# Three products of an expert in a row, and its weights split two stages ahead

## Chip, core and metric

One Trainium2 chip, of which the kernel uses one core. The metric is the device time of one execution in microseconds, lower is better. PE is the matmul engine (TensorE), ACT the ScalarE, DVE the VectorE, POOL the GpSimd; SP issues most of the DMAs.

## What is computed

Causal attention with a decay (4 batches, 8 heads, 576 positions of 64), then a dense layer pair, then a layer of 8 experts of which each token uses one. Only the last part is touched:

```python
e_idx = np.argmax(x @ w_gate, axis=1)          # x: 2304 x 512, 8 experts
for e in range(E):
    mask = e_idx == e
    h = np.maximum(x[mask] @ w1[e], 0.0)       # w1: 8 x 512 x 1024
    ye = h @ w2[e]                             # w2: 8 x 1024 x 512
    out[mask] = gate_w[mask, None] * eom[mask, e, None] * ye
```

## The kernel before

All matrices are held as a pair of 16-bit parts, high and low, so a product of two takes three matmuls for each 128x128 step. A float32 weight is brought in by SP (L867, tile `stw`, 512 KB, an eighth of an expert's weights: four for W1, four for W2), and *split*: ACT copies the high part (L879), DVE subtracts to get the low part (L880).

The experts' part works on lists of tokens, 128 to a block. An expert has up to three blocks in the first round. Block 0 of experts 0 and 1 is a reserved block that is done early, ahead of `round_`, with its operands and results in the tile `wi` of the dense layer, which is free by then (L1128 to L1132, L1158). For all others `gather` (L942) lets POOL fetch the rows of a block from DRAM into `xg` (L951, indirect DMA, three buffers), and SP transposes them into `xs` by DMA (L954, two buffers). `expert1` (L964), the first product, makes eight groups of 12 matmuls (L977), each in a PSUM bank; ACT (L980) and DVE (L981) evacuate a group into `hT`. The main blocks use the pool `ps2` with five banks, the third block `ps_mm` with three. `expert2` (L985), the second product, takes 24 matmuls of 512 columns for each block (L996), ACT scales the result into `y` (L1002), and POOL scatters it to the output (L1003, indirect DMA).

The third block (block 2) is done only if the expert has over 256 tokens (`when`, a branch at run time); in these inputs experts 0, 1, 4 and 6 have it. A second round for over 384 tokens does not run.

The order on PE, ACT and DVE is that of the code (`manual_schedule`); POOL and SP get theirs from the scheduler. `round_` runs the first product of expert e+1 (with its third block's both products), then gathers for e+2, then the second product of e. `weights_steps` (L844) is a generator: a step splits one part and issues the load three parts on (the ring `stw` has three buffers in the pool `wp`). `spread` takes such steps between the groups of a product, and what is left behind it. 16 parts, all weights of experts 0 and 1, are split ahead of `round_`. `xp` (L1165) is the pool of the experts' part; it opens where the dense layer's tiles close, so its tiles lie where those lay, and the framework makes their first users wait for the last users of what lay there.

Of the kernel before, what the change touches and what calls it, by code (L numbers as in the profile page):

```python
# [9 lines left out]
F32 = mybir.dt.float32  # L10
# [8 lines left out]
P = 128  # L19
# [39 lines left out]
def attention_moe_kernel(ctx: ExitStack, tc: tile.TileContext, q, k, v, f, w_in, w_out,  # L59
# [5 lines left out]
    E, _, F2 = w1.shape  # L65
    KD = DM // P
# [255 lines left out]
    st = {}  # L322
# [518 lines left out]

    def weights_steps(wp):  # L844

        parts, tiles = [], {}

        def add(e, which):
            wv = (w1, w2)[which][e].rearrange("(k p) f -> p k f", p=P)
            for i in range(KD):  # L850
                n = F2 // P // KD
                parts.append((wv[:, i] if which == 0 else wv[:, n * i:n * i + n], e, which,
                              i if which == 0 else slice(n * i, n * i + n)))

        for e, which in ((0, 0), (1, 0), (0, 1), (1, 1)):
            add(e, which)
        for e in range(2, E):
            add(e, 0)
            add(e, 1)
        sts = []  # L860

        def fetch():
            st = wp.tile([P, F2], F32, tag="stw", name="stw", bufs=3)
            src = parts[len(sts)][0]
            if len(src.shape) == 3:
                st = st.rearrange("p (a b) -> p a b", a=src.shape[1])
            nc.sync.dma_start(out=st, in_=src)  # L867
            sts.append(st)

        for _ in range(3):  # L870
            fetch()
        yield
        for i, (_, e, which, js) in enumerate(parts):
            if (e, which) not in tiles:
                tiles[e, which] = (wp.tile([P, 2, KD, F2], F16, tag="W1", name="W1", bufs=2) if which == 0 else
                                   wp.tile([P, 2, F2 // P, DM], F16, tag="W2", name="W2", bufs=2))
                wts[e, which] = tiles[e, which]
            hi, lo = (tiles[e, which][:, x, js] for x in range(2))
            nc.scalar.activation(out=hi, in_=sts[i], func=AF.Copy)  # L879
            nc.vector.tensor_tensor(out=lo.bitcast(BF16), in0=sts[i], in1=hi, op=ALU.subtract)  # L880
            if len(sts) < len(parts):
                fetch()
            yield
# [58 lines left out]
    def gather(e, pool, blocks, into=None):  # L942

        n = len(blocks)
        if into is None:
            xs = pool.tile([P, 2 * KD, NSB * P], F16, tag="xs2", name="xs2", bufs=2)[:, :, 0:n * P]
            xg = [pool.tile([P, 2 * DM], F16, tag="xg", name="xg", bufs=3) for _ in blocks]
        else:
            xs, xg = into[0], [into[1]]
        for j, s in enumerate(blocks):  # L950
            nc.gpsimd.indirect_dma_start(out=xg[j], out_offset=None,  # L951
                                         in_=rows[0:NT if into is None else NBL * P, :],
                                         in_offset=bass.IndirectOffsetOnAxis(ap=slot[s][0][:, e:e + 1], axis=0))
            nc.sync.dma_start_transpose(out=xs[:, :, j * P:(j + 1) * P], in_=xg[j])  # L954
            xs_t[e, s] = (xs, j * P)

    def h_tile(e, blocks, into=None):
        n = len(blocks)
        if into is None:
            into = xp.tile([P, F2 // P, 2, NSB * P], F16, tag="hT", name="hT", bufs=2)  # L960
        for j, s in enumerate(blocks):
            h_t[e, s] = (into, j * P)

    def expert1(e, ps_pool, blocks):  # L964

        W1, (xs, o) = wts[e, 0], xs_t[e, blocks[0]]
        hT, ho = h_t[e, blocks[0]]
        w = len(blocks) * P
        hs = slice(ho, ho + w)
        for m in range(F2 // P):  # L970
            ps = ps_pool.tile([P, 512], F32, tag="mm", name="mm")
            i = 0
            for j in range(KD):
                for a, b2 in ((0, 0), (0, 1), (1, 0)):
                    l = W1[:, a, j, m * P:(m + 1) * P]
                    r = xs[:, b2 * KD + j, o:o + w]
                    nc.tensor.matmul(ps[:, 0:w], lhsT=l.bitcast(BF16) if a else l, rhs=r.bitcast(BF16) if b2 else r,  # L977
                                     start=i == 0, stop=i == 3 * KD - 1)
                    i += 1
            nc.scalar.activation(out=hT[:, m, 0, hs], in_=ps[:, 0:w], func=AF.Relu)  # L980
            nc.vector.scalar_tensor_tensor(out=hT[:, m, 1, hs].bitcast(BF16), in0=ps[:, 0:w], scalar=0.0,  # L981
                                           in1=hT[:, m, 0, hs], op0=ALU.max, op1=ALU.subtract)
            yield

    def expert2(e, pool, ps_pool, blocks, into=None):  # L985

        W2 = wts[e, 1]
        NF2 = F2 // P
        for s in blocks:
            hT, ho = h_t[e, s]  # L990
            ps = ps_pool.tile([P, 512], F32, tag="mm", name="mm")
            i = 0
            for m in range(NF2):
                for a, b2 in ((0, 0), (0, 1), (1, 0)):
                    l, r = hT[:, m, a, ho:ho + P], W2[:, b2, m, :]
                    nc.tensor.matmul(ps, lhsT=l.bitcast(BF16) if a else l, rhs=r.bitcast(BF16) if b2 else r,  # L996
                                     start=i == 0, stop=i == 3 * NF2 - 1)
                    i += 1
                if m % 2 and m < NF2 - 1:
                    yield  # L1000
            y = pool.tile([P, DM], F32, tag="y", name="y", bufs=3) if into is None else into
            nc.scalar.activation(out=y, in_=ps, func=AF.Copy, scale=slot[s][2][:, e:e + 1])  # L1002
            nc.gpsimd.indirect_dma_start(out=out,  # L1003
                                         out_offset=bass.IndirectOffsetOnAxis(ap=slot[s][1][:, e:e + 1], axis=0),
                                         in_=y, in_offset=None, bounds_check=NT - 1, oob_is_err=False)
            yield


    def run(g, n=1):

        last = None
        for _ in range(n):
            r = next(g, "end")
            last = r or last
            if r == "end":
                break
        return last
# [10 lines left out]
    def adv():  # L1028
        with tc.high_priority(offset=ATTN_FIRST):
            r = next(at, "end")  # L1030
        nsteps[0] += 1
        return r != "end"
# [33 lines left out]
    wp = None  # L1066
    nw = 0

    def open_weights():
        nonlocal wp, wg_  # L1070
        while adv():
            pass
        attn_ctx.close()
        wp = ctx.enter_context(tc.tile_pool(name="wp", bufs=1, side="right"))
        wg_ = weights_steps(wp)

    for c in range(NCH):
# [13 lines left out]
        for _ in moe1_steps(c):  # L1091
# [24 lines left out]
            if c == NCH - 2 and wp is None and len(complete) == 3 * B:  # L1116
                open_weights()
# [21 lines left out]
    ps2 = ctx.enter_context(tc.tile_pool(name="ps2", bufs=5, space=PSUM))  # L1139

    first = [expert1(e, ps2, (0,)) for e in range(2)]
# [21 lines left out]
            more = nc.values_load(nrounds[0:1, 0:1], min_val=0, max_val=NT // CAP)  # L1163
    moe1_ctx.close()
    xp = ctx.enter_context(tc.tile_pool(name="xp", bufs=1))  # L1165

    def round_(first):
        main = [(1,) if first and e < 2 else (0, 1) for e in range(E)]

        def fetch(e):  # L1170
            blocks = main[e] + (2,)
            gather(e, xp, blocks)
            h_tile(e, blocks)

        def when(e):

            return tc.If(regs[e] > CAP - P) if first else nullcontext()

        def spread(g, n):

            done = 0
            for i, _ in enumerate(g):
                if done < n and i % 2 == 0:
                    run(wg)
                    done += 1
            run(wg, n - done)

        def first_product(e):
            spread(expert1(e, ps2, main[e]), KD if 1 < e else 0)
            with when(e):  # L1190
                for _ in expert1(e, ps_mm, (2,)):
                    pass
                for _ in expert2(e, xp, ps_mm, (2,)):
                    pass

        wg = wg_
        if not first:
            wg = weights_steps(wp)
            run(wg, 4 * KD + 1)
        fetch(0)  # L1200
        fetch(1)
        first_product(0)
        for e in range(E):
            if e + 1 < E:
                first_product(e + 1)
            if e + 2 < E:
                fetch(e + 2)
            spread(expert2(e, xp, ps2, main[e]), KD if e + 2 < E else 0)
# [41 lines left out]
```

## Time and profile before

| | us |
|---|---|
| median of 3 runs (824.41 to 963.61) | 827.16 |
| the profiled execution | 825.52 |
| its span | 823.7 |
| PE busy in it | 741.9 (90%) |
| ACT, DVE, POOL busy | 452.1, 467.9, 313.7 |

The span is the time from the first to the last instruction that the profile shows. The timeline merges neighbouring instructions of one kind into a row, so that a row is a stage or a piece of one; where an engine stood before a row, brackets give how long and what ended the wait. The experts' part begins at 606.85 us, and PE's last matmul there ends near 812.

### The profile page before, as it was taken

Reading aid. Unit: us, or ns where it says so; the run is one execution under the profiler, and the core shown is the slowest. Engines: PE = TensorE matmul, PEld = TensorE weight load, DVE = VectorE, ACT = ScalarE, POOL = GpSimd, SP = SyncE. Lnnn points to the kernel's source line nnn. Section 1 sums busy time; section 2 is a strip of 40 time slices with the busy share of each in tenths; the row PEclk is TensorE's granted clock in tenths of the full one; section 3 lists DMA queues with packets and bytes.
Section 4 is the critical chain, followed back from the end, with each engine's and each line's share of the span. In section 5 each row is a group of like instructions: output and inputs, shape, how many; then the busy total and the mean of one; then the engine's idle time right before and its main releaser. Section 6 shows DMA issues by size and latency. Waiting matters only on the chain. (4 is left out here: it accounts for less than half of the span.)

```text
span 823.7 us, 16593 instructions
## 1 busy us (share of the span) xinstructions
PE 741.9 (90%) x6177; PEld 476.7 (58%) x6177; DVE 467.9 (57%) x1267; ACT 452.1 (55%) x909; POOL 313.7 (38%) x393
## 2 busy tenths in 40 slices
PE   4755988979899999998999999999999879999994
PEld 2543455645566655565555666666877546767561
DVE  7998988548642864258524776750512455455330
ACT  4874879757883775378615655540222445455330
POOL 9546788855663453156413500010131222211101
PEclk9876999999999999999999999999999989999998
DMA  8758899989994783579524757511364798599411
GB/s 245 233 177 188 177 218 255 193 133 174 171 167 104 149 140 66 93 136 161 92 46 104 122 173 237 150 37 39 82 163 90 226 284 256 173 271 247 146 55 40
DMA packets 263778, 127.95 MB, mean 155 GB/s; under 512 B 214658, under 2 KB 247522, under 8 KB 263684
## 3 DMA queue, kind: packets, MB, share of 16 engines
q1 hardware_dynamic: 251860, 105.20, 58.3%
q0 software_dynamic: 4960, 15.73, 6.0%
q10 hardware_dynamic: 6864, 5.80, 2.6%
q8 instruction: 54, 0.88, 0.4%
q14 instruction: 40, 0.33, 0.1%
HBM read 71.52 MB, written 10.08 MB: 99 GB/s over the span
## 5 line engine op out<-in xcount | busy, mean ns | idle before, releaser
L695 PE MATMUL mm<-xT,wi 128*128 128x384 f16 (+1 forms) x1152 | 208.6, 328 | 8.2 <-DMA xT<-xn 5.0
L718 PE MATMUL mm<-g,wo 128*128 128x384 f16 (+1 forms) x1152 | 198.3, 326 | 1.5 <-DVE hr L702 1.4
L695 PEld LDWEIGHTS <-wi 128*128 128x128 f16 (+1 forms) x1152 | 110.5, 98 | 82.3 <-issue 13.0
L718 PEld LDWEIGHTS <-wo 128*128 128x128 f16 (+1 forms) x1152 | 111.0, 98 | 74.7 <-issue 3.8
L880 DVE TENSOR_TENSOR W<-stw,W 128x1024 bf16<-128x1024 f32 x64 | 77.7, 1224 | 68.5 <-ACT W L879 64.5
L977 PEld LDWEIGHTS <-W 128*128 128x128 f16 (+1 forms) x1344 | 100.7, 99 | 22.8 <-DVE W L880 5.4
L977 PE MATMUL mm<-xs,W 128*128 128x256 f16 (+3 forms) x1152 | 102.6, 250 | 9.1 <-ACT W L879 4.0
L394 POOL TENSOR_TENSOR pn<-ms,pn 128x384 bf16<-128x384 f32 (+1 forms) x80 | 82.7, 1039 | 56.1 <-ACT pn L393 50.7
L376 ACT ACTIVATE ms<-ms,nm 128x512 f32<-128x512 f32 (+4 forms) x144 | 79.5, 577 | 39.1 <-DVE nm L342 27.9
L996 PE MATMUL mm<-W,hT 128*128 128x512 f16 (+1 forms) x432 | 94.5, 379 | 0.6 <-PEq L1190 0.3
L879 ACT ACTIVATE W<-stw 128x1024 f16<-128x1024 f32 x64 | 66.6, 1052 | 30.4 <-DMA stw<-in_moe_w_dram 29.8
L342 DVE CUSTOM_DVE_ANT_1 ms<-sc,mask 128x128 f32<-128x128 f32 (+3 forms) x128 | 59.1, 484 | 26.2 <-PE sc L295 13.9
L707 DVE TENSOR_TENSOR g<-hr,g 128x384 bf16<-128x384 f32 x80 | 55.6, 697 | 32.0 <-ACT g L703 31.9
L996 PEld LDWEIGHTS <-hT 128*128 128x128 f16 (+1 forms) x432 | 41.8, 98 | 50.7 <-issue 1.6
L702 DVE SCALAR_TENSOR_TENSOR hr<-hr,mm 128x384 f32<-128x384 f32 x96 | 52.7, 549 | 27.9 <-ACT hr L699 27.4
L699 ACT ACTIVATE hr<-mm,bias 128x384 f32<-128x384 f32 x96 | 54.5, 568 | 17.8 <-PE mm L695 16.2
L703 ACT ACTIVATE g<-hr 128x384 f16<-128x384 f32 x96 | 49.4, 516 | 26.7 <-DVE hr L702 26.1
L1003 POOL DMA_INDIRECT out_dram<-y,ids x18 | 18.3, 1014 | 120.2 <-ACT y L1002 104.0
L981 DVE SCALAR_TENSOR_TENSOR hT<-mm,hT 128x128 bf16<-128x128 f32 (+1 forms) x96 | 32.9, 355 | 47.0 <-ACT hT L980 32.7
L428 PE MATMUL pv<-vt,pt 128*128 128x65 f16 x320 | 41.5, 197 | 18.4 <-DVE xs L453 9.9
L295 PE MATMUL sc<-K,q 128*128 128x256 f16 (+3 forms) x192 | 49.0, 297 | 7.6 <-DVE nm L342 7.0
L980 ACT ACTIVATE hT<-mm 128x128 f16<-128x128 f32 (+1 forms) x96 | 30.8, 329 | 42.0 <-PE mm L977 37.6
(189 smaller groups left out, 1121.3 us busy)
## 6 DMA issues: line engine op xcount, KB each, us to landing
stw<-in_moe_w_dram SPq DMA_DIRECT2D x64, 512.0 KB
wo<-in_moe_w_in_dram SPq DMA_DIRECT2D x16, 512.0 KB
raw<-in_moe_w_out_dram ACTq DMA_DIRECT2D x11, 512.0 KB
rows<-rw POOLq DMA_DIRECT2D x15, 256.0 KB, 3.6
ldk<-in_k_dram SPq DMA_DIRECT2D x14, 256.0 KB
ldq<-in_q_dram SPq DMA_DIRECT2D x14, 256.0 KB
ldv<-in_v_dram SPq DMA_DIRECT2D x13, 256.0 KB
g<-in_moe_w_out_dram SPq DMA_DIRECT2D x3, 512.0 KB
```

Source lines behind the costliest of these rows:

```text
L342: nc.vector.tensor_tensor_reduce(out=pairs(ms[:, off:off + w]), in0=ps[:, 0:w].rearrange("p (c j) -> p c j", c=2), in1=pairs(mask[:, 640 - ...
L376: nc.scalar.activation(out=ms[:, off:off + w], in_=ms[:, off:off + w], func=AF.Exp, scale=-1.0, bias=nm[:, i:i + 1])
L394: nc.gpsimd.tensor_tensor(out=lo.bitcast(BF16), in0=ms[:, 0:N], in1=hi, op=ALU.subtract)
L695: nc.tensor.matmul(ps[:, 0:w], lhsT=l.bitcast(BF16) if a else l, rhs=r.bitcast(BF16) if b2 else r, start=i == 0, stop=i == 3 * KD - 1)
L699: nc.scalar.activation(out=hr, in_=ps[:, 0:w], func=AF.Relu, bias=bias3)
L702: nc.vector.scalar_tensor_tensor(out=hr, in0=hr, scalar=6.0, in1=ps[:, 0:w], op0=ALU.min, op1=ALU.mult)
L707: either.tensor_tensor(out=g[:, m, 1, 0:w].bitcast(BF16), in0=hr, in1=g[:, m, 0, 0:w], op=ALU.subtract)
L718: nc.tensor.matmul(ps[:, 0:w], lhsT=l.bitcast(BF16) if a else l, rhs=r.bitcast(BF16) if b2 else r, start=i == 0, stop=i == 3 * NF - 1)
L879: nc.scalar.activation(out=hi, in_=sts[i], func=AF.Copy)
L880: nc.vector.tensor_tensor(out=lo.bitcast(BF16), in0=sts[i], in1=hi, op=ALU.subtract)
L977: nc.tensor.matmul(ps[:, 0:w], lhsT=l.bitcast(BF16) if a else l, rhs=r.bitcast(BF16) if b2 else r, start=i == 0, stop=i == 3 * KD - 1)
L996: nc.tensor.matmul(ps, lhsT=l.bitcast(BF16) if a else l, rhs=r.bitcast(BF16) if b2 else r, start=i == 0, stop=i == 3 * NF2 - 1)
```

## The change

The loads' ring is kept outside the generator: `stw_in` names a pool and a number of buffers, `wp` and 3 at first, `xp` and 4 from the opening of `xp` on. At the start of round one two more loads are issued, so five parts are under way or waiting. In `round_` each expert's first product, third block and second product follow one another, and the splits are taken from the first product of expert 1 on, to that of expert 6.

```diff
+    stw_in, fetches = [], []
+
     def weights_steps(wp):
...
         def fetch():
-            st = wp.tile([P, F2], F32, tag="stw", name="stw", bufs=3)
+            pool, bufs = stw_in
+            st = pool.tile([P, F2], F32, tag="stw", name="stw", bufs=bufs)
...
         for _ in range(3):
             fetch()
+        fetches.append(fetch)
         yield
...
         wp = ctx.enter_context(tc.tile_pool(name="wp", bufs=1, side="right"))
+        stw_in[:] = wp, 3
         wg_ = weights_steps(wp)
...
     xp = ctx.enter_context(tc.tile_pool(name="xp", bufs=1))
+    stw_in[:] = xp, 4
...
         def first_product(e):
-            spread(expert1(e, ps2, main[e]), KD if 1 < e else 0)
+            spread(expert1(e, ps2, main[e]), KD if 0 < e < E - 1 else 0)
...
         fetch(0)
         fetch(1)
-        first_product(0)
+        for _ in range(2 if first else 0):
+            fetches[0]()
         for e in range(E):
-            if e + 1 < E:
-                first_product(e + 1)
+            first_product(e)
             if e + 2 < E:
                 fetch(e + 2)
             spread(expert2(e, xp, ps2, main[e]), KD if e + 2 < E else 0)
```

On POOL, this is the order at the start of round one before; `out_dram<-wi` is the scatter of a reserved block (expert 0, then expert 1), `xg<-rows` a gather:

```order
L793 DMA rows<-wi 128x1024 x3
L951 DMA xg<-rows,ids 128x1024 x6
L1003 DMA out_dram<-wi,ids 2304x512
L951 DMA xg<-rows,ids 128x1024
L1003 DMA out_dram<-wi,ids 2304x512
L1162 TENSOR_LOAD cnt
```

And with the change, at the same place, in a list that also names what each waits for (DMASW is a completed DMA of POOL's, DMAHW one of SP's):

```order
L1007 DMA out_0_dram<-wi_98,ids_7779 2304x512 [waits DVE_49,Activation_49]
L1007 DMA out_0_dram<-wi_98,ids_7779 2304x512 [waits DMASW4_49,Activation_49]
L955 DMA xg_8588<-rows_100,ids_8297 128x1024 [waits DMASW3_49,DMASW5_49,DMASW2_49,DMASW7_49,DMASW1_49,DMAHW4_49,DMASW0_49,DMAHW5_49,DVE_49,PE_49]
L955 DMA xg_8589<-rows_100,ids_8297 128x1024
L955 DMA xg_8596<-rows_100,ids_8297 128x1024
L955 DMA xg_8597<-rows_100,ids_8297 128x1024 [waits DMAHW5_49,DMASW6_49]
```

Six gathers stood ahead of the first scatter and one between the two; now both scatters stand ahead of all gathers, and the second scatter waits for the first (DMASW4).

On SP, at the start of round one before (`xs<-xg` are the transposes):

```order
L1163 ISA x2
L954 DMA_TRANSPOSE xs_8587<-xg 128x8x128 x2
L954 DMA_TRANSPOSE xs_8595<-xg 128x8x128 x2
L1190 COMPARE_AND_BRANCH
L1190 UNCONDITIONAL_BRANCH x2
L954 DMA_TRANSPOSE xs_9145<-xg 128x8x128 x3
```

And with the change:

```order
L1168 ISA x2
L870 DMA stw<-in_moe_w_dram 128x1024
L870 DMA stw<-in_moe_w_dram 128x2x512 x3
L958 DMA_TRANSPOSE xs_8587<-xg 128x8x128 x2
L958 DMA_TRANSPOSE xs_8595<-xg 128x8x128 x2
L1196 COMPARE_AND_BRANCH
L1196 UNCONDITIONAL_BRANCH x2
L958 DMA_TRANSPOSE xs_8878<-xg 128x8x128 x3
L870 DMA stw<-in_moe_w_dram 128x2x512
L870 DMA stw<-in_moe_w_dram 128x1024 x2
```

Four loads now stand ahead of the first transposes.

On ACT, from the third block of expert 0 on, before (`hT` is an evacuation of a first product, `y` of a second one, `W<-stw` a split):

```order
L980 ACTIVATE hT<-mm 128x128 x8
L1002 ACTIVATE y<-mm,cf 128x512
L1190 UNCONDITIONAL_BRANCH x2
L980 ACTIVATE hT<-mm 128x128 x8
L1190 COMPARE_AND_BRANCH
L980 ACTIVATE hT<-mm 128x128 x8
L1002 ACTIVATE y<-mm,cf 128x512
L1190 UNCONDITIONAL_BRANCH x2
L879 ACTIVATE W_9163<-stw 128x1024 x2
L1002 ACTIVATE y<-mm,cf 128x512
L879 ACTIVATE W_9163<-stw 128x1024 x2
L980 ACTIVATE hT<-mm 128x256
```

And with the change:

```order
L1006 ACTIVATE y<-mm,cf 128x512
L1196 UNCONDITIONAL_BRANCH x2
L883 ACTIVATE W_8896<-stw 128x1024 x2
L1006 ACTIVATE y<-mm,cf 128x512
L883 ACTIVATE W_8896<-stw 128x1024 x2
L984 ACTIVATE hT<-mm 128x128
L883 ACTIVATE W_8951<-stw 128x1024
L984 ACTIVATE hT<-mm 128x128 x2
L883 ACTIVATE W_8951<-stw 128x1024
L984 ACTIVATE hT<-mm 128x128 x2
L883 ACTIVATE W_8951<-stw 128x1024
L984 ACTIVATE hT<-mm 128x128 x2
```

Expert 0's second product with its four splits now stands ahead of expert 1's first product, and that has four splits of its own among its eight groups. Up to the scatters of the reserved blocks, no engine's order differs but in line numbers.

## Rows read from the trace of the kernel before

**Rows 1.** Timeline of PE, 560 to 640: start, length, line, operation, count, idle time before.

```profile
606.85 11.31 PE L977 MATMUL mm<-xs,W 128*128 128x128 f16 x192
617.99 5.34 PE L996 MATMUL mm<-W,hT 128*128 128x512 f16 x24
623.17 4.41 PE L977 MATMUL mm<-xs,W 128*128 128x128 f16 x76
```

**Rows 2.** Timeline of PE, 630 to 823.

```profile
635.89 10.52 PE L996 MATMUL mm<-W,hT 128*128 128x512 f16 x48
646.25 0.82 PE L977 MATMUL mm<-xs,W 128*128 128x256 f16 x6
...
661.29 5.34 PE L996 MATMUL mm<-W,hT 128*128 128x512 f16 x24 [0.15 <-PEq L1190]
666.47 0.82 PE L977 MATMUL mm<-xs,W 128*128 128x256 f16 x6
...
672.59 11.50 PE L977 MATMUL mm<-xs,W 128*128 128x256 f16 x85 [0.66 <-DVE W L880]
684.24 10.52 PE L996 MATMUL mm<-W,hT 128*128 128x512 f16 x48 [0.15 <-PEq L1190]
694.60 16.09 PE L977 MATMUL mm<-xs,W 128*128 128x256 f16 x192
...
726.06 10.64 PE L977 MATMUL mm<-xs,W 128*128 128x256 f16 x96
...
747.21 1.15 PE L977 MATMUL mm<-xs,W 128*128 128x256 f16 x9
...
764.76 15.70 PE L996 MATMUL mm<-W,hT 128*128 128x512 f16 x72
```

**Rows 3.** Groups by line, 600 to 823: busy us, mean ns, idle before by releaser.

```profile
L977 PE MATMUL mm<-xs,W 128*128 128x256 f16 (+3 forms) x1152 | 102.6, 250 | 9.1 <-ACT W L879 4.0 <-DVE W L880 3.6 <-issue 1.3
...
L880 DVE TENSOR_TENSOR W<-stw,W 128x1024 bf16<-128x1024 f32 x48 | 58.3, 1224 | 59.6 <-ACT W L879 55.8 <-issue 3.1 <-DVEq L1190 0.6
...
L981 DVE SCALAR_TENSOR_TENSOR hT<-mm,hT 128x128 bf16<-128x128 f32 (+1 forms) x96 | 32.9, 355 | 47.0 <-ACT hT L980 32.7 <-ACT wi L1002 11.3 <-issue 1.7
```

**Rows 4.** Stretches of 2 us: PE, PEld, DVE, ACT, POOL busy, PEclk, DMA share, GB/s.

```profile
674.00:676.00 2.00, 2.00 (x12) 1.35 (x10) 0.80 (x1) 1.44 (x2) 0.00 (x0) 0.50 1.02 379
676.00:678.00 2.00, 2.00 (x16) 1.62 (x15) 0.77 (x3) 0.42 (x2) 0.00 (x0) 0.79 0.91 339
```

**Rows 5.** Timeline of POOL, 578 to 660.

```profile
595.17 0.99 POOL L951 DMA_INDIRECT xg<-rows,ids  x1 [2.69 <-ACT wi L980]
...
603.70 0.94 POOL L951 DMA_INDIRECT xg<-rows,ids  x1 [5.01 <-DMA xs<-xg]
...
607.61 1.02 POOL L1003 DMA_INDIRECT out_dram<-wi,ids  x1 [0.30 <-issue]
611.76 0.97 POOL L951 DMA_INDIRECT xg<-rows,ids  x1 [3.13 <-DMA out_dram<-wi,ids]
...
650.83 0.97 POOL L951 DMA_INDIRECT xg<-rows,ids  x1 [2.40 <-DMA xs<-xg]
```

**Rows 6.** Timeline of ACT, 600 to 823.7.

```profile
607.05 0.69 ACT L1002 ACTIVATE wi<-mm,cf 128x512 f32<-128x512 f32 x1 [5.18 <-issue]
...
641.86 1.99 ACT L879 ACTIVATE W<-stw 128x1024 f16<-128x1024 f32 x2
```

**Rows 7.** DMA issues, 595 to 700: count, median us from issue to landing.

```profile
xg<-rows,ids POOLq DMA_INDIRECT x19, 5.7
...
out_dram<-wi,ids POOLq DMA_INDIRECT x2, 4.0
```

**Rows 8.** Landing of all 20 scatters to the output.

```profile
DMA to landing us min/median/max: 2.7/3.0/4.0
```

**Rows 9.** Timeline of SP's queue, 578 to 660.

```profile
598.56 40.14 SPq L954 DMA_TRANSPOSE xs<-xg  x9
...
644.59 1.25 SPq L954 DMA_TRANSPOSE xs<-xg  x1
```

## Prediction

> **What bounds the kernel now.** I read the page first and then only the last quarter of the span, since nothing before the experts' part differs in the order of any engine. The page gives a span of 823.7 us; the execution's own time is 825.52, beside a median of 827.16. From 606.85 on, PE does nothing but experts 0 to 7, and its timeline shows them one behind the other [rows 1, 2]. A first product over two blocks is 96 matmuls of 128x256 and takes 10.64 us undisturbed (start 726.06). Where it takes longer, PE waits for the splits of the weights: the group of L977 sat idle 9.1 us, 4.0 ended by ACT's split (L879) and 3.6 by DVE's (L880) [rows 3]. Expert 2's first product runs from 646.25 to 661.29, 15.04 us, 4.40 too long; expert 3's from 666.47 to 684.24, 17.77, 7.13 too long. Expert 6 with its third block takes 17.55 (747.21 to 764.76) where expert 4's same 192 matmuls take 16.09 (694.60): 1.46 too long. Together **12.99 us** are lost to weights that are split one stage before their use. Not all of it is idle time: in 674 to 676 PE was busy throughout at a granted clock of 0.50, the lower level of 1.2 GHz, after the gaps just before, and in 676 to 678 the mean is 0.79 [rows 4].
>
> **What the change removes.** W1 of expert e+2 was split during expert e's second product and used at once; now expert e+1's two products, over 20 us, lie between. W2 gains a stage too. So I remove all 12.99 us. The same 64 splits and 64 loads remain. The first product of e is now followed by e's own second product, which needs hT; its matmuls take the eight hT tiles in order, and the last tile's ACT and DVE work lies under the 21 matmuls ahead of it (5.34 us for 24 [rows 1]). That edge costs nothing; if ACT were held there for over 4 us it would cost the excess.
>
> **What it adds, 1: the gathers go behind the scatters.** The two rows lists of POOL in the section on the change carry this. The loads' ring is now allotted from xp, so xg has moved. Before, the first three gathers for round one stood ahead of the scatters of experts 0 and 1 (reserved block, tile wi); the first began at 595.17, under the reserved block's products [rows 5]. Now both scatters stand first, and the first gather names the semaphores of scatters and of PE among its waits: xg lies where wi lay. POOL runs in order, so:
> - expert 1's y leaves ACT at 607.05 + 0.69 = 607.74 [rows 6]; with the 0.30 that POOL takes between two issues [rows 5] its scatter starts at 608.0.
> - That scatter must land: 4.0 us, as the two from wi took; the least of all scatters is 2.7 [rows 7, 8]. The gather that was released by the first one began at 607.61 + 4.0 + 0.15 = 611.76 [rows 5]. So the first gather starts at 612.2.
> - From gather to SP's transpose: 595.17 to 598.56, 3.39 us without weight loads [rows 5, 9]; 5.7 is the median landing in the whole stretch with loads [rows 7].
> - From the transpose to its landing: 598.56 to 603.70, 5.14, without loads; 644.59 to 650.83, 6.24, with them [rows 5, 9].
> PE can start expert 0 at 620.7 by the unloaded rows, at 624.1 by the loaded ones. Four loads are released by the same scatter and stand ahead of the transposes on SP, but they end early in the chain; I take the middle, 622.4. PE began at 606.85 with no wait before [rows 1], so it stands **15.55 us** (12.5 with the landing of 2.7; 17.25 at most). No gain is possible here: work only moves later.
>
> The Trainium skill, "DMA: Bandwidth & Descriptors", section "Anatomy of one DMA — SWDGE (gpsimd) path", fits such a DMA as 2.0 us plus its bytes over 436 GB/s, which is 2.6 us for 256 KB. An estimate by that page for the scatter and the gather would start PE at about 618.5 and give 829.3. The trace disagrees, with 4.0 and 3.39 to 5.7, so the rows stand in my sum.
>
> **2: the clock.** After such a stop the matmuls begin at the lower level. After expert 3's gaps PE ran without a break from 672.59 [rows 2], and at half clock until 676.84, if the 0.79 of the slice from 676 on [rows 4] is 0.42 of it at half: 4.2 us, half of it lost, **2.1 us**. The lower end is 0 (the level is kept), the upper the same 2.1, for each restart is alike.
>
> **3: splits in a narrow first product.** Expert 1's first product (one block, 128 wide) has four splits of W2 among its eight groups, where it had none; two splits of W1 are left over behind expert 0's second product. The ACT lists in the section on the change show both. A group is 12 matmuls, 0.70 us (192 in 617.99 - 606.85 = 11.14 [rows 1]). On DVE: y, 0.69, and two ACT splits, 1.99 [rows 6], and a DVE split of 1.22 put the start 4.2 us late with PE's answer time; eight evacuations of 0.36 and four splits of 1.22 [rows 3] are 7.8. DVE then reaches the third block at about 12.0, and its first evacuation ends near 12.3. PE has five and three PSUM banks, so its twelfth group needs that bank, and would be there at 11 x 0.70 = 7.7: **4.6 us** late. Before, this stretch already had gaps: 623.17 to 635.89 is 12.72, 1.58 over 11.14 [rows 1, 2]; they fall into the new wait. I take 3.0 net; ends 4.6 and -1.6. The wider products do not suffer: there PE needs 10.64 for what is some 8 us of DVE.
>
> **Sum.** 825.52 - 12.99 + 15.55 + 2.1 + 3.0 = **833.2 us**.
>
> **Rivals.**
> - *The stop is covered.* If the scatter's release did not hold the first gather, experts would start as before: 833.2 - 15.55 - 2.1 = 815.5. For it: only block one of expert 0 is needed at first. Against: the POOL list alone puts the gather behind a scatter that cannot start before 608.0. Chance 0.10.
> - *The weights stay late; the change does not do what it says.* A single-pass expert moves 4.2 MB of weights in 21 us beside gathers and transposes, and in 674 to 676 the queues already show a share of 1.02 and 379 GB/s [rows 4]. If half the wait stays, 6.5 us come back: 839.7. Against: experts 4 and 5 ran without loss at that traffic with a ring of three [rows 2]. Chance 0.10.
> - *Slower by over 2%.* On SP the last load of each second product stands behind transposes that wait for the first product's end. Its split is ACT's fourth there, some 7.9 us on, and five banks of 1.33 us hide 6.6 more. A load that takes over 14.5 us then stops ACT, and evacuation and PE with it. At 17.5 us each of five experts loses 3: 848. Against: 2.1 MB at 379 GB/s take 5.5 us. The Trainium skill, same page, section "Queues, rings and completion order", says that a ring's descriptors are consumed in order; by it a load behind a transpose is late by all that stands ahead, and this is the rival it speaks for; at 379 GB/s it stays under the 14.5 us. Chance 0.08.
>
> **How the numbers follow.** Forecast 0.72, rivals 0.10, 0.10, 0.08. The forecast's own bounds: 825.52 - 12.99 + 12.5 + 0 - 1.6 = 823.4 and 825.52 - 12.99 + 17.25 + 2.1 + 4.6 = 836.5. The range takes in the second rival with its upper end, 824 to 842; the first and the third are left out, nearly 2 in 10. Over 2%, about what a measurement of this kernel can tell from no change, means below 810.6 or above 843.7. Faster needs the first rival and more, 0.02; slower the third and a tail, 0.10; within 2%, 0.88.
>
> **What would show it.** In the changed profile PE should stand from about 607 to 622, the wait ended by the transposes into xs, with the first gather at about 612 and a granted clock of 0.5 behind the stop. Expert 1's first product should take about 15 us instead of 12.7. Experts 2 and 3 should take 10.6 us each, expert 6 about 16.1, and no wait of L977 for L879 or L880 should remain there. I am wrong on the stop if the gathers start before 607, on the gain if experts 2 and 3 still take over 12 us, and on step 3 if expert 1 takes 11 to 12.7.

## Result and profile after

| | before | with the change |
|---|---|---|
| median, us | 826.15 (5 runs, 824.41 to 963.61) | 832.77 (5 runs, 829.80 to 834.32) |
| the profiled execution, us | 825.52 | 829.80 |
| its span, us | 823.7 | 828.1 |
| mean granted clock of PE in it | 0.969 | 0.957 |

The ratio is 1.0081, with a 95% interval of 1.0052 to 1.011: the change costs 0.8%. The prediction was 833.2 us and no change beyond 2%. The one disturbed run of before, 963.61, is in none of the ratios.

PE's timeline from the reserved block's second product to the end (start, length, line, operation, count; in brackets the idle time before and what ended it). L977, L996, L879, L880, L951, L954 and L1003 of before are L981, L1000, L883, L884, L955, L958 and L1007 here; the evacuations on ACT and DVE, L980 and L981 of before, are L984 and L985.

```profile
594.67 10.53 PE L1000 MATMUL mm<-W,wi 128*128 128x512 f16 x48
621.63 12.19 PE L981 MATMUL mm<-xs,W 128*128 128x128 f16 x192 [16.43 <-DMA xs<-xg]
633.65 10.52 PE L1000 MATMUL mm<-W,hT 128*128 128x512 f16 x48
644.01 3.51 PE L981 MATMUL mm<-xs,W 128*128 128x128 f16 x60
648.49 0.83 PE L981 MATMUL mm<-xs,W 128*128 128x128 f16 x12 [0.97 <-DVE hT L985]
649.83 3.51 PE L981 MATMUL mm<-xs,W 128*128 128x128 f16 x60 [0.50 <-DVE hT L985]
654.61 3.51 PE L981 MATMUL mm<-xs,W 128*128 128x128 f16 x60 [1.28 <-DVE hT L985]
657.96 10.52 PE L1000 MATMUL mm<-W,hT 128*128 128x512 f16 x48
668.32 10.64 PE L981 MATMUL mm<-xs,W 128*128 128x256 f16 x96
679.11 10.52 PE L1000 MATMUL mm<-W,hT 128*128 128x512 f16 x48
689.47 10.64 PE L981 MATMUL mm<-xs,W 128*128 128x256 f16 x96
700.26 1.46 PE L1000 MATMUL mm<-W,hT 128*128 128x512 f16 x6
702.21 9.22 PE L1000 MATMUL mm<-W,hT 128*128 128x512 f16 x42 [0.49 <-ACT W L883]
711.27 16.05 PE L981 MATMUL mm<-xs,W 128*128 128x256 f16 x192
...
763.85 16.05 PE L981 MATMUL mm<-xs,W 128*128 128x256 f16 x192
779.74 15.70 PE L1000 MATMUL mm<-W,hT 128*128 128x512 f16 x72
```

Expert 0 began at 606.85 with no wait in [rows 1]; here PE stands for 16.43 us. Expert 1 (644.01 to 657.96) has three gaps that DVE ends. Experts 2 and 3 (668.32, 689.47) run their 96 matmuls without a wait, 10.79 us from start to next start where [rows 2] had 15.04 and 17.77, and expert 6's 192 take 15.89 where it had 17.55.

The stop on POOL's timeline, then on the queue of SP, then on ACT, from 598 to 626:

```profile
606.20 1.00 POOL L1007 DMA_INDIRECT out_dram<-wi,ids  x1 [4.17 <-ACT wi L1006]
610.02 0.99 POOL L955 DMA_INDIRECT xg<-rows,ids  x1 [2.82 <-issue]
```

```profile
609.35 1.84 SPq L870 DMA_DIRECT2D stw<-in_moe_w_dram  x4
617.24 9.31 SPq L958 DMA_TRANSPOSE xs<-xg  x4
```

```profile
605.24 0.69 ACT L1006 ACTIVATE wi<-mm,cf 128x512 f32<-128x512 f32 x1 [4.50 <-PE mm L1000]
```

ACT finishes expert 1's y at 605.93, POOL starts its scatter at 606.20, and only behind it do SP's four loads (609.35) and the first gather (610.02) start. The gather's transpose starts at 617.24, and 4.39 us later PE goes on. In [rows 5] the gather stood at 595.17, ahead of the scatters.

The groups by line from 600 to 828 (busy us, mean ns, idle before by releaser):

```profile
L981 PE MATMUL mm<-xs,W 128*128 128x256 f16 (+3 forms) x1152 | 98.2, 248 | 19.2 <-DMA xs<-xg 16.4 <-DVE hT L985 2.7
L1000 PE MATMUL mm<-W,hT 128*128 128x512 f16 (+1 forms) x432 | 94.7, 379 | 1.1 <-ACT W L883 0.5
...
L883 ACT ACTIVATE W<-stw 128x1024 f16<-128x1024 f32 x48 | 49.4, 1050 | 6.7 <-DMA stw<-in_moe_w_dram 6.3 <-ACTq L1196 0.4
```

The 7.6 us that L977 waited for the splits in [rows 3] are gone from L981; 0.5 is left, on a second product. In their place stands the one wait of 16.4.

The granted clock behind the stop (stretch, PE, PEld, DVE, ACT and POOL busy, PEclk, DMA share, GB/s):

```profile
608.00:620.00 12.00, 0.00 (x0) 0.00 (x0) 0.00 (x0) 0.00 (x0) 2.93 (x3) 0.50 0.85 265
...
623.00:625.00 2.00, 2.00 (x26) 2.00 (x25) 0.58 (x2) 0.56 (x2) 1.43 (x2) 0.65 0.52 139
625.00:627.00 2.00, 2.00 (x39) 2.00 (x37) 0.79 (x3) 0.83 (x3) 0.46 (x1) 1.00 0.73 174
```

The clock is at its lower level (0.50, 1.2 GHz) from 608 on, while PE stands, and back at 1.00 by 625.

**The balance.** From the end of the reserved block to PE's last matmul, before takes 205.1 us (606.85 to about 812) and after 211.4 (605.20 to 816.59): 6.3 more. By pieces, from start to next start: the stop 16.43; expert 0's first product 633.65 - 621.63 = 12.02 against 11.14 [rows 1], 0.88; expert 1's 657.96 - 644.01 = 13.95 against 12.72, 1.23; the late weights -12.9 (15.04, 17.77 and 17.55 of [rows 2] against 10.79, 10.79 and 15.89); expert 3's second product 0.65 longer (11.01 against 10.36 for expert 2's). The sum is 6.3.

### The profile page after: what moved, and what is told of

Read it like the earlier page. It is cut to its first block, busy times and chain, and to the rows that moved or that the text cites. A ratio compares the mean times of both kernels' runs of the same rounds, so it can differ in the third digit from the quotient of the medians.

```text
span 828.1 us, 16598 instructions
## 1 busy us (share of the span) xinstructions
PE 738.6 (89%) x6177; PEld 477.7 (58%) x6177; DVE 466.0 (56%) x1267; ACT 450.5 (54%) x909; POOL 314.8 (38%) x393
## 5 line engine op out<-in xcount | busy, mean ns | idle before, releaser
L695 PE MATMUL mm<-xT,wi 128*128 128x384 f16 (+1 forms) x1152 | 211.4, 331 | 7.9 <-DMA xT<-xn 5.2
L981 PEld LDWEIGHTS <-W 128*128 128x128 f16 (+1 forms) x1344 | 101.1, 99 | 28.2 <-issue 20.0
L981 PE MATMUL mm<-xs,W 128*128 128x256 f16 (+3 forms) x1152 | 98.2, 248 | 19.2 <-DMA xs<-xg 16.4
L884 DVE TENSOR_TENSOR W<-stw,W 128x1024 bf16<-128x1024 f32 x64 | 77.3, 1224 | 58.3 <-ACT W L883 57.7
L1000 PE MATMUL mm<-W,hT 128*128 128x512 f16 (+1 forms) x432 | 94.7, 379 | 1.1 <-ACT W L883 0.5
L883 ACT ACTIVATE W<-stw 128x1024 f16<-128x1024 f32 x64 | 66.3, 1052 | 21.6 <-DMA stw<-in_moe_w_dram 21.2
L985 DVE SCALAR_TENSOR_TENSOR hT<-mm,hT 128x128 bf16<-128x128 f32 (+1 forms) x96 | 33.0, 355 | 74.7 <-ACT hT L984 72.5
L1000 PEld LDWEIGHTS <-hT 128*128 128x128 f16 (+1 forms) x432 | 41.8, 98 | 51.3 <-ACT W L883 1.2
L1007 POOL DMA_INDIRECT out_dram<-y,ids x18 | 18.7, 1038 | 119.0 <-ACT y L1006 102.4
L984 ACT ACTIVATE hT<-mm 128x128 f16<-128x128 f32 (+1 forms) x96 | 31.1, 331 | 53.9 <-PE mm L981 53.8
```

## Experiments

The kernel before ran with each kernel on the same chip, and the ratios are to it; its medians there lay between 830.6 and 831.4 us.

**Where the stop comes from.** The built program shows where the tiles lie, in bytes of a partition. `wi` begins at 97120. `xp` ends at 88448 before, with the change at 104832, because the ring's 16 KB push up what is allotted behind it. What reaches into `wi` is only `RA` and the tables of the second round, which doesn't run. `xg` itself lies at 36704 in both. (These places are read from the program; no trace shows them.) So my sentence that `xg` had moved onto `wi` was wrong, and two theories were left. A: a pool that overlaps `wi` anywhere is held as a whole until `wi`'s last user is done. B: the new order of the code or SP's loads put the gathers behind. The first run takes `RA` and the tables out of `xp`, which then ends at 89952.

```diff
+    xr = ctx.enter_context(tc.tile_pool(name="xr", bufs=1))
-        RA = xp.tile([P, NB, CAP], F16, name="RA")
+        RA = xr.tile([P, NB, CAP], F16, name="RA")
-            table(RA, 0, xp, ps_mm, range(NSB), NB)
+            table(RA, 0, xr, ps_mm, range(NSB), NB)
```

> The change, with one edit: RA and the tables of the second round (which does not run) get a pool of their own, so that xp ends at 89952 bytes, below 97120 where wi begins. In the changed kernel xg lies where it lay before (36704 to 42848), but xp as a whole grew from 88448 to 104832 and so reached into wi. Theory A (the whole pool waits for the last user of anything below it): the first gather is back near 595 us, PE has no stop of 16 us, and the gain of 13 us stays: 826.15 - 12.99 + 1.2 (expert 1's first product, 13.95 instead of 12.72) = about 815, 814 to 818. Theory B (as my prediction put it, the tile xg itself was moved onto wi, or the scheduler merely put the scatters first): the tile's place is the same as in the changed kernel, so the stop stays and the time is about 832.

Measured: 821.26 us (6 runs), ratio 0.9898 [0.9873, 0.9923]. PE's timeline:

```profile
610.59 4.12 PE L981 MATMUL mm<-xs,W 128*128 128x128 f16 x71 [1.27 <-DMA xs<-xg]
...
624.20 10.52 PE L1000 MATMUL mm<-W,hT 128*128 128x512 f16 x47
634.56 3.56 PE L981 MATMUL mm<-xs,W 128*128 128x128 f16 x60
...
648.79 10.52 PE L1000 MATMUL mm<-W,hT 128*128 128x512 f16 x47
```

The stop has shrunk from 16.43 to 1.27 us with the order of the products and the code of the loads as they were: A holds, B falls. The gain is smaller than theory A had it (814 to 818 beside 826.15, a ratio near 0.987): the first gather comes at 602.76 and not near 595, against the reserved block's end 5.1 us later than before. What holds it there is taken up below. The other way round, the kernel before gets one unused tile of 16 KB in `xp`, which then ends at 104832.

```diff
+        pad = xp.tile([P, 4 * F2], F32, name="pad")
+        nc.gpsimd.memset(pad[:, 0:1], 0.0)
```

> The kernel before, with one unused tile of 16 KB added to xp, so that this pool alone reaches into wi; order, splits and loads are those of before. Theory A: the stop arises here too, without any other part of the change: scatter at about 607.6, landing 2.8 us later, 0.7 to the gather, 3.4 to the transpose and 5.1 to its landing is 619.6, so PE stands some 13 us, with up to 1 us of slower clock behind it: 837 to 842. Theory B: no stop, 826.

Measured: 844.13 us (4 runs), ratio 1.0183 [1.0149, 1.0217]. Its PE, POOL and SP timelines:

```profile
622.43 12.55 PE L977 MATMUL mm<-xs,W 128*128 128x128 f16 x192 [13.03 <-DMA xs<-xg]
```

```profile
614.24 1.00 POOL L951 DMA_INDIRECT xg<-rows,ids  x1 [2.82 <-issue]
```

```profile
618.03 9.27 SPq L954 DMA_TRANSPOSE xs<-xg  x4
```

An unused tile makes a stop of 13.03 us, with no other part of the change. It is 3.4 us shorter than with the change, and all of that lies between the gather and its transpose: 614.24 to 618.03, 3.79 us, against 610.02 to 617.24, 7.22; from the transpose to PE it is 4.40 and 4.39. With the change four loads of 512 KB start 0.7 us ahead of the gather, and the DMAs carry 267 to 404 GB/s between 610 and 618 where here they carry 10 to 176 between 614 and 618. It is the gathers themselves that land late, as the list of DMA issues says, with the median us to landing at the end of the line; first the changed kernel (609.3 to 613), then the padded one (613.5 to 618):

```profile
xg<-rows,ids POOLq DMA_INDIRECT x3, 7.7
```

```profile
xg<-rows,ids POOLq DMA_INDIRECT x3, 4.0
```

SP's transposes wait for that landing and not for SP's own loads. The gather comes from POOL's queue and the loads from SP's, so it is not behind them in a queue. The Trainium skill, "DMA: Bandwidth & Descriptors", section "Queues, rings and completion order", says that each DMA engine takes the queues with work for it in turn, packet by packet; the two gathers agree with it.

The third run drops the two extra loads of the change, to see those 3.4 us come back.

```diff
-        for _ in range(2 if first else 0):
+        for _ in range(0):
```

> The change without the two extra loads at the start of round one (the ring of four in xp stays, the splits follow three parts behind the loads). It tells what the loads ahead of the first transposes cost in the stop, where the changed kernel took 7.2 us from the first gather to its transpose against 3.4 before. If the loads cause it: the stop is 3 to 4 us shorter, 12.5 to 13.5 instead of 16.4, and the time 828 to 831. If they don't: 16 us as before, 832 to 835.

Measured: 836.28 us (5 runs), ratio 1.0074 [1.0041, 1.0108], with a stop of 16.36. SP's queue:

```profile
619.54 1.84 SPq L870 DMA_DIRECT2D stw<-in_moe_w_dram  x4
627.01 9.68 SPq L958 DMA_TRANSPOSE xs<-xg  x4
```

There are still four loads ahead: the new ring's buffers are all free, so the first four loads go at once whenever the code asks for them. The edit didn't do what it was meant to. Its first gather starts at 620.21, again 0.7 us behind the loads, and takes 6.80 us to its transpose. So the two kernels with loads just ahead of the gather have 7.22 and 6.80, and the ten without have 3.3 to 3.8. No run takes the loads alone out of the stop: that they are the cause is argued from this, not shown. What the run does show is that the two extra loads in the change do nothing that the time tells, 1.0074 beside 1.0081, though ACT's waits for loads sum to 16.9 us here and to 6.3 with them.

**What brings the 13 us: order or ring?** The next two runs each have one of them. Order alone, with the ring of three in `wp`:

```diff
-            spread(expert1(e, ps2, main[e]), KD if 1 < e else 0)
+            spread(expert1(e, ps2, main[e]), KD if 0 < e < E - 1 else 0)
-        first_product(0)
         for e in range(E):
-            if e + 1 < E:
-                first_product(e + 1)
+            first_product(e)
```

> The order of the stages and the splits of the change, on the ring of three loads in wp of before; no more loads, xp as before. Theory A (the order by itself brings the gain, the ring costs the stop): no stop, experts 2 and 3 at 10.6 us each, expert 1 near 14: 814 to 818. Rival (the four-deep ring is needed, or ACT stands on late loads and the evacuations behind it): 818 to 824, with first products of experts 2 and 3 over 12 us.

Measured: 827.31 us (12 runs), ratio 0.9951 [0.9927, 0.9976]. Two of its groups by line:

```profile
L977 PE MATMUL mm<-xs,W 128*128 128x256 f16 (+3 forms) x1152 | 99.5, 248 | 12.9 <-DVE hT L981 10.3 <-ACT y L1002 2.1 <-issue 0.5
...
L879 ACT ACTIVATE W<-stw 128x1024 f16<-128x1024 f32 x48 | 49.9, 1053 | 38.1 <-DMA stw<-in_moe_w_dram 36.5 <-DVE W L880 1.3 <-ACTq L1190 0.2
```

PE no longer waits for weights, but it waits 12.9 us all the same: ACT stands 36.5 us on loads that are not there yet, and the evacuations queue behind it. The time is that of the rival, but its sign came out in part: expert 2's first product takes 10.98 us and is not held, expert 1's takes 17.69, expert 3's 13.93 and expert 4's 20.04 (15.92 in [rows 2]). From the late load on this is the third rival of the prediction, with a ring of three. Why the loads are late, because they stand behind transposes on SP as it said or because no buffer of the ring is free, was not told apart. Then the ring alone: the order of before, ring of four in `xp`, the extra loads, and `RA` in its own pool so that no stop is in play.

```diff
+    stw_in[:] = xp, 4
+        for _ in range(2 if first else 0):
+            fetches[0]()
-        RA = xp.tile([P, NB, CAP], F16, name="RA")
+        RA = xr.tile([P, NB, CAP], F16, name="RA")
```

> The kernel before with the ring of four and the two more loads, but its own order of the products; the second round's lists lie in a pool of their own, so that no stop is in play. Theory A (order and ring are both needed: two of the four splits of W1 of expert 2 still stand just ahead of their use): expert 2's first product stays about 4 us too long, expert 3's shrinks from 7.1 to about 3, expert 6's 1.5 goes; the start loses about 4 us as in the changed kernel with the split pool; ratio 0.992 to 1.000. Rival (only the loads were late, the order is of no account): experts 2 and 3 take 10.6 each, ratio 0.988 to 0.992. Rival (the ring is of no account): experts 2, 3 and 6 as before, ratio 1.00 to 1.006.

Measured: 829.63 us (10 runs), ratio 1.0001 [0.9977, 1.0025]. PE, around expert 3's first product:

```profile
673.07 0.82 PE L981 MATMUL mm<-xs,W 128*128 128x256 f16 x6
675.00 0.39 PE L981 MATMUL mm<-xs,W 128*128 128x256 f16 x2 [1.12 <-ACT W L883]
...
688.41 10.52 PE L1000 MATMUL mm<-W,hT 128*128 128x512 f16 x47
```

With the loads early and the order old, experts 2 and 3 each still take 15.3 us (652.54 to 667.89, 673.07 to 688.41), 4.5 too long, since the last two splits of their W1 stand right ahead of their use; only expert 3's surplus over that (2.4 of its 7.1, where I expected 4) and expert 6's 1.5 go. What that gains, the start loses again: expert 0's first product waits 1.78 us for its rows and takes 13.23 instead of 11.14. So order and ring are both needed: 0.5% by order alone, nothing by the ring alone (the loss at the start is in it), 1.0% by both without the stop.

**What the ring costs at the start, and step 3.** With the split pool, expert 0 still loses 1.27 us of waiting and its first product takes 13.61 instead of 11.14. In that run SP issues three loads at 585.48, ahead of the transposes into `wi` from which POOL writes the rows, and the first gather comes at 602.76. In the next version the ring's four loads are all asked for at the start of the round, and held until the first transpose into `xs` has been issued; in its trace they go behind the fourth.

```diff
-            nc.sync.dma_start(out=st, in_=src)
+            with tc.issue_after(hold[-1]) if hold else nullcontext():
+                nc.sync.dma_start(out=st, in_=src)
...
+            if into is None and not held:
+                hold.append(t.ins)          # t: the transpose into xs
...
-        for _ in range(2 if first else 0):
+        for _ in range(4 if first else 0):
```

> The changed kernel with the split pool, and the ring's first four loads held until the first block's transpose into xs has been issued. Theory (the four loads that SP issues ahead push the writes and transposes of the rows back, and with them the gathers by 7 us): the first gather starts near 595 to 597 again, expert 0's first product begins without a wait and takes 11.1 to 12.0 us in place of 13.6 after a wait of 1.3; 2 to 4 us below the split pool alone, ratio 0.985 to 0.988. Rival (loads that start later are late for their splits): a wait of the first product for the splits comes in at expert 1 or 2, and the time is that of the split pool alone or above, 0.990 or more.

Measured: 819.01 us (6 runs), ratio 0.9864 [0.983, 0.9899]; a second time, on another chip: 817.87 us (6 runs), 0.9825 [0.9792, 0.9858].

> The version with the split pool and the held loads once more, for a comparison on the same chip with the one whose narrow first product is free of splits. All theories: ratio 0.984 to 0.989, expert 1's first product and third block 14 to 15 us.

SP's queue, in the first of the two:

```profile
586.05 3.99 SPq L791 DMA_TRANSPOSE wi<-x  x3
601.62 9.27 SPq L959 DMA_TRANSPOSE xs<-xg  x4
610.93 2.18 SPq L871 DMA_DIRECT2D stw<-in_moe_w_dram  x4
```

The three transposes into `wi` take 3.99 us where they took 7.24 between the loads, the first gather stands at 598.03, and expert 0 begins without a wait. Its first product takes 12.40 (11.16 the second time), where up to 12.0 was expected, and 10.86 and 11.43 in the two later runs with held loads; with loads ahead it took 13.0 to 13.6 in three runs (in the run of the order alone, with none ahead, 12.25). Expert 1's takes 14.5 both times: no PE wait is for a split, though ACT waits 1.46 us for the load of the fourth split there, and DVE 0.49 behind it. By the medians the first of the two is 2 us below the split pool alone, the size that was expected; its interval and that of the split pool alone overlap, that of the second lies below.

Step 3 said that DVE sets the length of expert 1's narrow first product. Two edits test it. One lets POOL make four of its low parts, with the split pool alone and with the held loads too:

```diff
-            nc.vector.tensor_tensor(out=lo.bitcast(BF16), in0=sts[i], in1=hi, op=ALU.subtract)
+            (nc.gpsimd if 20 <= i < 24 else nc.vector).tensor_tensor(out=lo.bitcast(BF16), ...)
```

> The changed kernel with the split pool, and the low parts of four splits (expert 2's W2, those among expert 1's first product) made by POOL in place of DVE. Step 3 of the prediction says that DVE, with eight evacuations and four splits, sets the length of this narrow first product: then expert 1's first product and third block go from 14.2 us to 11.2 to 12.5, and the time is 1.5 to 2.5 us below that of the split pool alone (821.3 beside 830.8 of the kernel before): ratio 0.986 to 0.988. Rival (ACT or the loads set it): 14 us as it was, and the same time as with the split pool alone, 0.990.

> The two edits of the runs beside it together: loads held behind the first transpose, and four low parts on POOL. If both theories hold and the gains add, the experts' part loses some 13 us against the kernel before, ratio 0.982 to 0.986; if they share one wait (a late start hides the splits' work), it is that of the better one alone, 0.985 to 0.988.

Measured: 820.93 us (4 runs), ratio 0.9889 [0.984, 0.9939], and 819.00 us (6 runs), 0.9878 [0.9845, 0.991]: neither differs from its version without the edit, and the gains don't add. The group on POOL and three rows of PE, in the first:

```profile
L884 POOL TENSOR_TENSOR W<-stw,W 128x1024 bf16<-128x1024 f32 x4 | 8.5, 2143 | 1.4 <-issue 1.4
```

```profile
648.70 10.52 PE L1001 MATMUL mm<-W,hT 128*128 128x512 f16 x47
659.06 8.02 PE L982 MATMUL mm<-xs,W 128*128 128x256 f16 x72
669.64 2.78 PE L982 MATMUL mm<-xs,W 128*128 128x256 f16 x24 [2.56 <-DVE hT L986]
```

Expert 1's stage shrinks from 14.23 to 12.94 us (635.76 to 648.70), and with the held loads from 14.54 to 13.13, so DVE did hold it. It does not get down to the 11.2 to 12.5 that were expected: with DVE relieved, ACT waits 1.02 us for the load of its fourth split there, and the evacuations and PE with it. And POOL takes 2.14 us for what DVE does in 1.22, and expert 2's first product now waits 2.56 (1.51 with the held loads): the wait has moved on by one expert. There ACT stood 4.78 us on a load. That the load was late because POOL freed the ring's buffers late fits, and was not tried apart. The other edit leaves the narrow product free of splits and lets them end one stage later, in expert 6's second product:

```diff
-            spread(expert1(e, ps2, main[e]), KD if 0 < e < E - 1 else 0)
+            spread(expert1(e, ps2, main[e]), KD if 1 < e < E - 1 else 0)
-            spread(expert2(e, xp, ps2, main[e]), KD if e + 2 < E else 0)
+            spread(expert2(e, xp, ps2, main[e]), KD if e + 1 < E else 0)
```

> The version with the split pool and the held loads, but the splits are taken from expert 2's first product on, and to expert 6's second product: expert 1's narrow first product has none. Theory (step 3 of the prediction: four splits among eight narrow groups, with the evacuations, set the length of that product): it and the third block go from 14.7 us to about 12.5, the 12.7 of the kernel before, where two left-over splits still stand ahead of it; later stages keep 10.6 and 16.05 us, since every split still has a product between it and its use; 2 us below the version with the splits there, ratio about 0.984 where that has 0.986. Rival (the work only moves): with one stage less of lead a wait for the splits comes in at a first or second product from expert 2 on, and the time is the same.

Measured: 815.40 us (6 runs) where before has 831.44, ratio **0.98 [0.9767, 0.9834]**. PE:

```profile
627.88 3.61 PE L984 MATMUL mm<-xs,W 128*128 128x128 f16 x60
632.36 7.53 PE L984 MATMUL mm<-xs,W 128*128 128x128 f16 x132 [0.87 <-DVE hT L988]
639.73 10.52 PE L1003 MATMUL mm<-W,hT 128*128 128x512 f16 x47
```

Expert 1's stage takes 11.85 us instead of 14.45 on the same chip, and no later one grows: the splits in this product are what made it long, as step 3 said, and the rival (the work only moves) falls. That DVE is the engine that holds it there rests on the run before this and on DVE's own timeline in the changed kernel, which has no gap from 645.88 to the eighth evacuation. By the medians this is 2.5 us; the intervals of the two overlap, so it is the trace that tells them apart, not the times. From the reserved block's end to the last matmul this version takes 191.6 us where before took 205.1. By the ratios, 0.98 and 1.0081 on two chips, it beats both kernels.

## Why the prediction came out

The time agrees, 833.2 against a median of 832.77, but that is partly luck and flatters the sum. The sum was made for a profiled execution, and after's profiled one took 829.80, the fastest of its five. There the experts' part grew by 6.3 us where the sum said 7.7. The other 1.9 us are outside what was costed: the reserved block ended 1.65 us earlier (in the runs above this point lies anywhere from 605 to 615), and the tail was 0.2 shorter.

- **The gain, 12.99.** Right: 12.9, with the ring and the order both at work, and 0.65 given back in one second product. (My three terms set distances from start to start against the length of a row: 10.64 us of a row are 10.80 to the next start, 16.09 are 15.92. Two terms are 0.16 too large by it and the third 0.17 too small, so the sum hardly moves.) I counted the ring as nothing but a shift of the loads. The order alone shows that without it most of the gain turns into evacuations late behind ACT.
- **The stop, 15.55.** Right in size (16.43): the scatter started 1.0 us and the first gather 4.8 us behind the reserved block's end, where 1.15 and 5.35 were worked out. Its cause was named wrongly: not `xg` has moved, the pool as a whole is held by its topmost, unused tiles. The order of before and after on POOL showed the wait itself, which is why the number survived. Two terms were off in opposite directions: the scatter held the gather for 3.82 us and not 4.2, and from the gather to PE it was 11.61 and not 10.2, 3.4 more than in the padded kernel up to the transpose, most likely because of the four loads; I had written that they end early in the chain. And the 3.82 are near the 4.2 by luck: the scatter landed in 2.8 us and not in 4.0 (only one of the two of before has a landing in the trace), and 1.0 us more passed until the gather, where 0.15 was counted.
- **The clock, 2.1.** Too large for this execution. PE was at the lower level only until about 624.4, and the 192 matmuls took 0.88 us longer than in [rows 1]. The 11.14 of [rows 1] hold small waits of their own: from 625 on, after's 12 matmuls of a group follow one another every 0.67 us, 10.7 for 16 groups, so the lower level itself cost about 1.3 of the 12.02. I had taken the restart behind expert 3's gaps [rows 4] for the pattern, "each restart is alike"; that one lasted 4.2 us, this one 2.8, the one behind expert 2's gaps in the same trace of before 2.4 (650.53 to about 652.9). In the run without the two extra loads it lasted 5.4 us behind a stop as long (16.36), and the 192 matmuls took 13.26, 2.1 more than in [rows 1]. So restarts are not alike, and the 2.1 lies within their spread; what sets their length stays open.
- **Step 3, 3.0 net.** The mechanism was right, the size was not: 1.23, so 13.95 us instead of 15. The place was right in part: the twelfth group waits for its bank (1.28 us), but the sixth and seventh do so before it (0.97, 0.50), as the first five groups have taken the five banks of the main block. Together they put the twelfth group 2.9 us late (10.6 behind the start, against 7.7) and not 4.6. The start of DVE's evacuations, 4.2 us late, was right. But for the eight evacuations I took 0.36 us each from a group of mixed shapes [rows 3]. The narrow ones take 0.288, and two in a row 0.48. The eighth main evacuation ended near 10.4 us after the start and not at 12.
- **The rivals.** *The stop is covered*: no; PE needs the first gather at once. *The weights stay late*: no; L981 has no wait for a split, at up to 396 GB/s between 674 and 678. *Slower by over 2%*: that late loads stop ACT, and PE with it, is real, as the order alone shows, but the ring of four holds it off. ACT's waits for loads sum to 6.3 us here, the longest 2.02 before 690, against 36.5 with the ring of three.

The change is thus a gain of some 13 us that a stop of 16 hides; without the stop it is 0.9898, and with two smaller edits 0.98.

## What to carry to other kernels

A tile added to a pool that opens over another's memory costs not only its bytes: look up where the pool now ends and who used that memory last, also for tiles that only a branch never taken needs. When weights are split earlier, the loads must come earlier by as much, or the waiting engine passes its delay on to the evacuations behind it. Price an operation from a row of its own shape, and keep large loads from starting just ahead of a small transfer that the path waits for.

## What the runs showed that I had not expected

- With four loads of 512 KB started 0.7 us ahead on another queue, gathers landed in 7.7 us (median of three) and the first had its transpose after 7.22; without them it was 4.0 and 3.79. That the loads are the cause was not tried apart.
- After a stop of 13 to 16 us at the granted clock 0.50, PE stayed at that level for another 2.8 us (changed kernel), 3.5 (padded kernel) and 5.4 (without the two extra loads). The 192 matmuls took 12.02, 12.39 and 13.26 us against 11.14 in the kernel before: 0.9, 1.25 and 2.1 more. Against 10.7, at the 0.67 us a group that all of them reach at the full clock, it is 1.3, 1.7 and 2.5.
- In the first expert's first product of several kernels PE stands 0.2 to 1.0 us at a time with nothing in the profile to wait for, for example 617.08 in the run with the split pool, at a full clock. It is absent behind the stops of 13 to 16 us, but not behind the wait of 1.27 us in that run; and it is absent in the run with held loads and POOL's low parts, where PE had not stood. Its cause stays open.
